# Weight-conversion units, attention bursts and fold fetches placed anew in a one-core chain of retention and two MoE layers

## The chip, the cores and the metric

The kernel runs on one core of a Trainium2 chip. The metric is device time in microseconds, the median of the runs; a profiled execution gives the trace. The engines are named PE (matrix multiply; PEld its weight loads), DVE (vector), ACT (scalar activation), POOL (GpSimd) and SP (which here issues every DMA). SPq is SP's queue of DMA issues, L99 the one helper line from which all of them come.

## The reference

```
scores = matmul(q, k^T) / sqrt(64)             # 8 x 8 heads, 576 positions, width 64
ret    = matmul(scores * gamma^(i-j), v)       # lower triangle only
x      = ret as 4608 x 512
h      = max(x @ w1, x @ w2, x @ w3)           # moe,  512 -> 768
x      = h @ w_out                             # 768 -> 512
a, b   = x @ w1, x @ w2                        # moe2, 512 -> 1024
out    = ((a * b) @ w3) @ w_out                # 1024 -> 1024 -> 512
```

Weights arrive as float64 and are turned into float32 words on the chip.

## The kernel before, in words

**First stage (to about 494 us).** Tokens go in 9 blocks of 512. For every block, 18 products (6 slices f of the hidden width, 3 weights i) of 12 matmuls each make `ps_h`; ACT copies the first of three into `hb`, DVE takes the maximum with the other two (L502), and `hb` is stored to `h_d`. One product is one tick of a list, `plan`: `when(t, fn)` puts a step at a time counted in ticks, the list is sorted, and every engine gets its instructions in that order and works through them strictly in order. Blocks 0 and 1 are written out by hand in the string `ORDER`, where a `+` takes the next step from the sorted list; tick 36 is where block 2 starts.

**Attention** is computed chunk by chunk in bursts of two chunks (`attend`, with `t_o` the tick at which a burst's outputs are made and `behind` that of the burst ahead of it, where its scores are made). A chunk fetches q and k (eight DMAs, L99), POOL scales q and v, DVE transposes them to `qt` and `kt` (L368), PE makes the scores `sc`, the outputs `o` and the new state `st`, DVE turns `st` into the state `s` (two instructions, L416 and L418) and masks the scores (`p`, L382). PSUM tiles `ps_h`, `sc` and `st` share six banks in turn, so a `sc` waits until the `hb` step has read the `ps_h` that had its bank six tiles before.

**Conversion units.** The late weights (moe w_out, moe2 w1, w2, w_out, w3) are 46 units of 512 KB. Each is fetched as raw words 6 ticks ahead (`fetch`), split by ACT (two instructions, L172 and L173), combined by DVE in three instructions (L177, L178 `CUSTOM_DVE`, L181; the order listing calls L178 ISA), and stored to DRAM. The last 16 units are moe2's w3, which is also transposed (L235) before its store to `w3t_d`. The queue of SP issues all of this in order, and a store waits there until DVE has made its data.

**Second stage.** After the moe product, w3 and w_out of moe2 are folded into one matrix (`ps_w`; operands `th`, `tl`, `oh`, `ol` are split from `raw`), then seven-product forms of the two moe2 products follow (`ps_x`, `ps_v`, `ps_y`); their operands, `t4l` among them, are split by the steps of `operands`, each low half being made by the engine that `split` names.

Of the kernel before, what the change touches and what calls it, by code (L numbers as in the profile page):

```python
# [22 lines left out]
P = 128  # L23
N1 = 512
KF1, KF2, KD = F1 // P, F2 // P, DM // P
EARLY = 2
# [13 lines left out]
ga8 pr0.9 ft14 xh7 lo10 ft15 xl7 kp0.2 ft16 up8 ou8 mx0.9 + + + pr0.10 xh8 xl8 + pr1.0 mx0.10 sl11 jn11 wo13 pr1.2  # L40
sl12 ft17 mx1.0 sl13 hi11 wo14 lo11 pr1.6 sl14 wo15 jn12 wo16 jn13 pr1.3 jn14 mx1.6 hi12 hi13 lo12 hi14 pr1.1 lo13
mx1.3 lo14 sl15 jn15 wo17 pr0.11 mx1.1 hi15 mx1.2 lo15 kp1.0 sl16 pr1.5 mx0.11 jn16 kp0.3 sl17 hi16 pr1.4 lo16 jn17
hi17 pr1.9 mx1.4 mx1.5 lo17 kp1.1 pr0.12 mx1.9 pr1.7 mx0.12 + + + mx1.7 + + + + pr1.8 + + + + + + pr0.15 mx1.8 + + +
kp1.2 pr0.17 + + + + pr0.16 mx0.15 + mx0.16 + + mx0.17 kp0.5 + + + + + + + + pr0.14 + + + pr1.10 + + + + + + + +
pr0.13 mx1.10 pr1.12 mx0.13 + + mx0.14 + kp0.4 + + + + pr1.11 mx1.12 + + mx1.11 + + + kp1.3 + + + + + + + pr1.15 + + +
+ + + + + + + pr1.16 mx1.15 + + + + pr1.13 + + + + mx1.16 pr1.14 mx1.13 + + + + pr1.17 mx1.14 + kp1.4 + + + + + + +
mx1.17 + kp1.5 + + + + + + + + + + + + + + + + + + +
"""
BACC = dict(dynamic_dma_scratch_size=512)

# [37 lines left out]
def tile_retention_maxout_bilinear(ctx: ExitStack, tc, a, out):  # L88
    nc = tc.nc
# [8 lines left out]
    def load(dst, src):  # L98
        nc.sync.dma_start(out=dst, in_=src)  # L99
# [11 lines left out]
    w3t_d = dram.tile([P, KF2, KF2, P], F32, name="w3t_d")  # L111
# [42 lines left out]
    n_blk = NT // N1  # L154
    T_BLK = 3 * KF1


    def convert(t, loads, done, name=None):

        z = {}  # L160

        def fetch():
            z["raw"] = cv.tile([P, 1024], I32, tag="raw", name="raw", bufs=6)
            for dst, src in loads(z["raw"]):
                load(dst, src)

        def words():
            raw = z["raw"].rearrange("p (n t) -> p n t", t=2)
            z["hi"] = raw[:, :, 1]
            z["e"] = cv.tile([P, 512], F32, tag="e", name="e")  # L170
            z["r"] = cv.tile([P, 512], I32, tag="r", name="r")
            nc.scalar.activation(z["e"], raw[:, :, 1].bitcast(F32), AF.Copy, scale=2.0 ** -112)  # L172
            nc.scalar.activation(z["r"], raw[:, :, 0].bitcast(U32), AF.Copy, scale=2.0 ** -29)  # L173

        def scale():
            z["m"] = cv.tile([P, 512], I32, tag="m", name="m", bufs=4)
            nc.vector.tensor_scalar(z["m"], z["e"].bitcast(I32), 3, None, ALU.logical_shift_left)  # L177
            nc.vector.tensor_tensor(z["m"], z["m"], z["r"], ALU.add)  # L178

        def join():  # L180
            nc.vector.scalar_tensor_tensor(z["m"], z["hi"], -0x80000000, z["m"], ALU.bitwise_and, ALU.bitwise_or)  # L181
            z["w"] = z["m"].bitcast(F32)

        def finish():
            done(t, z["w"])

        if name is None:
            when(t - 6, fetch)
            when(t - 1, words)
            when(t, scale)  # L190
            when(t + 1, join)
            t += 2
            when(t, finish)
        else:
            for kind, fn in (("ft", fetch), ("wo", words), ("sl", scale), ("jn", join)):
                early(kind + name, fn)
            for kind, fn in (("hi", done[0]), ("lo", done[1])):
                early(kind + name, lambda fn=fn: fn(z["w"]))

    def words_of(name):  # L200
        return a[name].bitcast(I32)
# [21 lines left out]
    def rows_unit(t, src, dst):  # L223
        convert(t, lambda raw: [(raw, src)], lambda t, w: load(dst, w))

    def w3_unit(t, j, half):
        src = words_of("moe2_w3")[512 * half:512 * half + 512].rearrange("(b r) e -> r b e", r=32)

        def loads(raw):
            r = raw.rearrange("p (b e) -> p b e", e=64)  # L230
            return [(r[32 * e:32 * e + 32], src[:, :, 64 * (4 * j + e):64 * (4 * j + e) + 64]) for e in range(4)]

        def done(t, w):
            wt = cv.tile([P, 512], I32, tag="m", name="m", bufs=4).bitcast(F32)
            nc.vector.transpose(out=wt, in_=w)  # L235
            load(w3t_d[:, j, 4 * half:4 * half + 4], wt.rearrange("p (m i) -> p m i", i=P))

        convert(t, loads, done)

# [2 lines left out]
    rest = [lambda t, k=k: rows_unit(t, words_of("moe_w_out")[k * P:(k + 1) * P], wo1_d[:, k]) for k in range(KF1)]  # L242
# [2 lines left out]
        for i in range(2) for c in (0, 2, 1, 3) for half in range(2)]  # L245
    rest += [lambda t, k=k: rows_unit(t, words_of("moe2_w_out")[k * P:(k + 1) * P], wo2_d[:, k]) for k in range(KF2)]
    rest += [lambda t, j=j, half=half: w3_unit(t, j, half) for j in range(KF2) for half in range(2)]
    for u, add in enumerate(rest):
        add(EARLY * T_BLK - 4 + u * ((n_blk - 1 - EARLY) * T_BLK - 1) / len(rest))

# [216 lines left out]
    bursts = []  # L469
    for m in reversed(range(0, len(due), 2)):  # L470
        some = due[m:m + 2]
        t_o = min(some[-1][2], T_BLK * some[0][1] - 2.52, bursts[0][0] - 7 if bursts else NT)
        bursts.insert(0, (int(t_o + 0.52) - 0.52, some))
    behind = bursts[0][0] - 9
    for t_o, some in bursts:
        pair = {}
        for slot, (n, _, _) in enumerate(some):
            attend(n, behind, t_o, slot, pair)
        behind = t_o
# [28 lines left out]
    for t in range(n_blk):  # L508
        for f in range(KF1):
            for i in range(3):  # L510
                k = T_BLK * t + 3 * f + i
                if t < EARLY:
                    split = t == 0 and 3 * f + i < HALVED
# [16 lines left out]
    KH, half = KF1 // 2, DM // 2  # L530
# [104 lines left out]
    with tc.manual_schedule():  # L635
# [78 lines left out]
        steps = halves[0][:2] + halves[1][:1] + halves[0][2:] + halves[1][1:]  # L714
# [48 lines left out]
                    split()  # L763
            pending.append([get(n) for get, n in gets])

        first_34 = [((get_w3t, 0), (get_wo2, 0)), ((get_w3t, 1),), ((get_w3t, 2), (get_wo2, 1)), ((get_w3t, 3),)]

        def open_34():
            t34["p"] = t34x.enter_context(tc.tile_pool(name="t34", bufs=2, side="left"))
# [19 lines left out]
        for j, (_, _, _, size) in enumerate(z_groups):  # L789
# [25 lines left out]
            if j == 3:  # L815
# [4 lines left out]
                steps = [lambda gets=gets: prepare_34(*gets) for gets in first_34]  # L820
# [11 lines left out]
        behind = []  # L832
# [13 lines left out]
        def operands(j, dst, c):  # L846

            w, size = {}, z_groups[j][3]

            def fetch():  # L850
                lows()
                r = raw_z()[:, :, :, :size]
                for kk in range(2):
                    load(r[:, kk], z_d[j][:, 2 * kk + c].rearrange("p (e t) -> p e t", e=2))
                for e in range(2):
                    for kk in range(2):
                        w[f"b{kk + 1}{e + 1}"] = r[:, kk, e]

            def split(x, src, eng):
                h, l = (v[:, c, columns(size)] for v in ops[dst][x])  # L860
                w_src = w[src]
                copy_r(h, w[src])
                behind.append(lambda: low(eng, l, w_src, h))

            def sub(x, y, to=None):
                if to is None:
                    t = spare_z()[:, :size]
                else:
                    t = w[to]
                nc.vector.tensor_tensor(t, w[x], w[y], ALU.subtract)  # L870
                return t

            def diff(dst, x, y, to=None):
                if to:
                    lows()
                w[dst] = sub(x, y, to)

            return [fetch,
                    lambda: (split("b11", "b11", nc.gpsimd), diff("t3", "b22", "b12")),
                    lambda: split("b21", "b21", nc.gpsimd),  # L880
                    lambda: diff("t1", "b12", "b11", "b12"),
                    lambda: diff("t2", "b22", "t1"),
                    lambda: split("t1", "t1", nc.vector),
                    lambda: split("t2", "t2", nc.vector),
                    lambda: diff("t4", "b21", "t2", "b21"),
                    lambda: split("t3", "t3", nc.vector),
                    lambda: split("b22", "b22", nc.vector),
                    lambda: split("t4", "t4", nc.gpsimd)]

        def waiting():  # L890
            pass
# [7 lines left out]
        rest = []  # L899

        def fetches(j):
            steps = both(j)
            rest.append(steps[2:])
            return steps[:2]
# [2 lines left out]
            return [lambda two=steps[n:n + 2]: [step() for step in two] for n in range(0, len(steps), 2)]  # L907

        one, two = fetches(0)
        steps = [waiting, waiting, one, waiting, waiting, two] + rest.pop() + fetches(1) + 3 * [waiting]  # L910
        w4x = ctx.enter_context(ExitStack())
        w4_p = t34["late"] = w4x.enter_context(tc.tile_pool(name="w4", bufs=4, side="right"))
        ps_w = []
        for n in range(2 * KF2):
            k, e = divmod(n, 2)
# [215 lines left out]
        for n, (k, q) in enumerate(visits):  # L1131
            B, size = ops[k % 2], z_groups[k][3]
            if n == 5:
                steps = steps + fetches(visits[7][0])
            elif n == 9:
                steps = steps + late[1]
            elif n != 4:
                steps = steps + rest.pop()
# [41 lines left out]
            for o in (2 * q, 2 * q + 1):  # L1180
# [3 lines left out]
                def add(ps, x, y, start):  # L1184
                    for i in range(2):
                        (ah, al), (bh, bl) = wsum[i][q][x], B[y]
                        product(ps[i][:, :size], [(ah[:, c, fs], al[:, c, fs], bh[:, c, columns(size)], bl[:, c, columns(size)]) for c in range(2)],
                                start, True, not start)
# [134 lines left out]
```

## Time and profile before

| | |
|---|---|
| median of 3 runs | 1223.95 us (1223.43 to 1228.09) |
| profiled execution | 1223.12 us, span of its instructions 1221.4 us |
| PE busy | 1208.2 us, 99% of the span |
| DVE, ACT, POOL busy | 906.2, 506.1, 311.9 us |
| mean granted PE clock | 0.999 of full speed |

Idle time of an engine that is not the bottleneck costs nothing by itself. Matmul ends are modelled, so the places where PE really stood still are read from the waits and the timeline of PE.

### The profile page before, as it was taken

The numbers are of one execution on the slowest core, as the hardware profiler recorded it, in microseconds if no ns is written. First come the engines' busy times: TensorE is split into PE (matmuls) and PEld (weight loads), VectorE is DVE, ScalarE is ACT, GpSimd is POOL, SyncE is SP. The second block draws the span as 40 slices with busy tenths as digits, with TensorE's granted clock in tenths as the row PEclk, the third lists the DMA queues.
The fourth block names the chain that finished last, engine by engine and source line by source line (L and its number), as shares of the span: only waits on it lengthen the run. The fifth ranks groups of instructions, "written<-read, shape, count | busy, mean of one in ns | idle before, by whom it ended". The sixth has DMA issues, their size and how long they took to land.

```text
span 1221.4 us, 22975 instructions
## 1 busy us (share of the span) xinstructions
PE 1208.2 (99%) x8900; PEld 1078.7 (88%) x8900; DVE 906.2 (74%) x1256; ACT 506.1 (41%) x873; POOL 311.9 (26%) x262
## 2 busy tenths in 40 slices
PE   8999999999999989999999999999999999999999
PEld 6888888888888878888889888888998888999998
DVE  5996677777877767366998467876666777998996
ACT  4651222233222322234556454443443344555554
POOL 2211221121211110000000125545244442344443
PEclk9999999999999999999999999999999999999999
DMA  9955788887998787444753733333333314455553
GB/s 219 252 127 121 161 204 230 196 213 180 223 221 172 168 172 192 146 128 165 227 185 122 251 112 130 129 121 119 107 115 136 128 59 159 155 165 166 176 169 104
DMA packets 323793, 199.34 MB, mean 163 GB/s; under 512 B 241634, under 2 KB 279266, under 8 KB 323684
## 3 DMA queue, kind: packets, MB, share of 16 engines
q1 hardware_dynamic: 323684, 197.87, 57.9%
q8 instruction: 70, 1.15, 0.4%
q14 instruction: 39, 0.32, 0.1%
HBM read 131.76 MB, written 66.06 MB: 162 GB/s over the span
## 4 chain that ended last, share of the span: by engine, by line
PE 88%; DVE 3%; DMA 3%; SPq 3%; issue 1%; POOL 1%; ACT 1%; DVEq 0%; POOLq 0%; ACTq 0%
PE ps_h L492 29%; PE ps_x L723 22%; PE ps_y L723 11%; PE ps_v L723 6%; PE ps_X L723 5%; PE ps_w L723 3%; SPq L99 3%; PE ps_Y L723 3%; PE o L390 2%; PE sc L375 2%; PE ps_V L723 1%; PE st L410 1%; PE o L397 1%; DMA q<-in_q_dram 1%; DMA raw<-in_moe_w_dram 1%
## 5 line engine op out<-in xcount | busy, mean ns | idle before, releaser
L492 PE MATMUL ps_h<-xh,w1h 128*128 128x512 f32 (+1 forms) x664 | 250.2, 378 | 0.0
L492 PE MATMUL ps_h<-xh,w1l 128*128 128x512 f32 (+1 forms) x664 | 247.4, 374 | 0.0
L492 PE MATMUL ps_h<-xl,w1h 128*128 128x512 f32 (+1 forms) x664 | 167.1, 374 | 0.0
L492 PEld LDWEIGHTS ps_h<-xh,w1h 128*128 128x128 f32 x664 | 125.5, 189 | 19.7 <-issue 2.1
L492 PEld LDWEIGHTS ps_h<-xh,w1l 128*128 128x128 f32 x664 | 125.6, 189 | 16.8 <-issue 0.3
L492 PEld LDWEIGHTS ps_h<-xl,w1h 128*128 128x128 f32 x664 | 123.7, 189 | 16.9
L1177 POOL TENSOR_TENSOR c<-c 128x512 f32<-128x512 f32 (+1 forms) x60 | 83.3, 1389 | 164.8 <-DVE c L1169 127.4
L502 DVE TENSOR_TENSOR hb<-ps_h,hb 128x512 f32<-128x512 f32 (+1 forms) x110 | 74.4, 677 | 62.8 <-PE ps_h L492 59.1
L1164 ACT ACTIVATE snap<-ps_x 128x512 f32<-128x512 f32 (+1 forms) x100 | 55.3, 554 | 151.4 <-PE ps_x L723 139.7
L361 POOL TENSOR_TENSOR q<-q,tables 128x512 f32<-128x512 f32 (+1 forms) x31 | 31.7, 1023 | 295.5 <-DMA q<-in_q_dram 224.9
L93 ACT ACTIVATE hb<-ps_h 128x512 f32<-128x512 f32 (+1 forms) x56 | 32.7, 584 | 173.7 <-PE ps_h L492 171.5
L172 ACT ACTIVATE e<-raw 128x512 f32<-128x512 f32 x64 | 54.1, 845 | 52.3 <-DMA raw<-in_moe_w_dram 35.4
L93 ACT ACTIVATE xh<-o 128x512 fp32r<-128x512 f32 (+1 forms) x40 | 22.1, 552 | 116.2 <-PE o L397 77.9
L368 DVE STREAM_TRANSPOSE qt<-q 128x512 f32<-128x512 f32 (+1 forms) x31 | 40.8, 1315 | 29.4 <-POOL q L361 29.4
L364 POOL TENSOR_TENSOR v<-v,tables 128x512 f32<-128x512 f32 x40 | 45.6, 1142 | 61.7 <-DMA v<-in_v_dram 44.4
L382 DVE TENSOR_TENSOR p<-sc,mask 128x512 f32<-128x512 f32 (+1 forms) x80 | 48.0, 627 | 11.2 <-PE sc L375 11.1
L178 DVE CUSTOM_DVE_ANT_0 m<-m,r 128x1024 uint16<-128x1024 uint16 x64 | 48.2, 753 | 6.9 <-ACT r L173 0.2
L96 POOL TENSOR_TENSOR ol<-raw,oh 128x512 fp32r<-128x512 f32 x1 | 1.3, 1265 | 203.7 <-DMA raw<-w3t_d 203.7
L173 ACT ACTIVATE r<-raw 128x512 int32<-128x512 uint32 x64 | 53.2, 831 | 0.0
L181 DVE SCALAR_TENSOR_TENSOR m<-raw,m 128x512 int32<-128x512 int32 x64 | 50.7, 796 | 0.2
L1169 DVE TENSOR_TENSOR c<-ps_x,snap 128x512 f32<-128x512 f32 (+1 forms) x40 | 25.1, 634 | 32.6 <-ACT snap L1164 13.3
L368 DVE STREAM_TRANSPOSE kt<-k 128x512 f32<-128x512 f32 (+1 forms) x31 | 41.0, 1324 | 8.7 <-DMA k<-in_k_dram 8.6
(302 smaller groups left out, 3257.9 us busy)
## 6 DMA issues: line engine op xcount, KB each, us to landing
zr<-g_d SPq DMA_DIRECT2D x18, 1024.0 KB, 6.1
raw<-in_moe_w_dram SPq DMA_DIRECT2D x34, 512.0 KB, 5.8
g_d<-c SPq DMA_DIRECT2D x64, 256.0 KB, 2.2
zr<-z_d SPq DMA_DIRECT2D x28, 512.0 KB, 6.5
h_d<-hb SPq DMA_DIRECT2D x54, 256.0 KB, 3.5
b<-h_d SPq DMA_DIRECT2D x16, 768.0 KB, 5.9
out_dram<-ob SPq DMA_DIRECT2D x35, 256.0 KB, 2.1
v<-in_v_dram SPq DMA_DIRECT2D x32, 256.0 KB, 4.7
```

What stands on the lines that cost most here:

```text
L93: nc.scalar.activation(dst, src, AF.Copy)
L172: nc.scalar.activation(z["e"], raw[:, :, 1].bitcast(F32), AF.Copy, scale=2.0 ** -112)
L173: nc.scalar.activation(z["r"], raw[:, :, 0].bitcast(U32), AF.Copy, scale=2.0 ** -29)
L178: nc.vector.tensor_tensor(z["m"], z["m"], z["r"], ALU.add)
L181: nc.vector.scalar_tensor_tensor(z["m"], z["hi"], -0x80000000, z["m"], ALU.bitwise_and, ALU.bitwise_or)
L368: nc.vector.transpose(out=z[x + "t"][:, :, :c].rearrange("p h (t T) -> p T h t", T=r), in_=z[x][:, :r])
L382: nc.vector.tensor_tensor(z[g][:c, :, :c], z["sc"][g][:c, :, :c], mask[:c, :c].unsqueeze(1).to_broadcast([c, G, c]), ALU.mult)
L492: nc.tensor.matmul(ps[:, cols], l, r, start=n == 0, stop=n == len(mms) - 1)
L502: nc.vector.tensor_tensor(hb, unwoven(ps[:, cols]), hb, ALU.max)
L723: nc.tensor.matmul(ps, l, r, start=start and j == 0, stop=stop and j == len(mms) - 1, skip_group_check=again)
L1164: nc.scalar.activation(t, unwoven(ps[:, :size]), AF.Copy)
L1177: nc.gpsimd.tensor_tensor(x, x, y, ALU.mult)
```

## The change

Four things. The late units start at tick 18.5 in place of 32 and end at about the same tick; a unit of w3 gets five parts of the stretch where the others get four (3.0 ticks against 2.4; all had 2.33). A unit of w3 is fetched by one DMA with pieces of 1 KB instead of four with pieces of 256 bytes; DVE's transpose writes its output in another order, and the store becomes four DMAs of 32 partitions. A burst comes at most 8 ticks behind the one ahead of it: from tick 51.48 to 131.48 the bursts stand 8 ticks apart, where gaps of 11, 7, 9, 7, 8, 9, 7, 7, 7, 8 ticks stood. In the fold, `wo2` 1 is fetched one step earlier, the second fetch of the first moe2 operands too, and the low halves of `t4` in the first group are made on DVE instead of POOL.

```
-hi17 pr1.9 mx1.4 mx1.5 lo17 kp1.1 pr0.12 mx1.9 pr1.7 mx0.12 + + + mx1.7 + + + + pr1.8 + + + + + + pr0.15 mx1.8 + + +
+hi17 pr1.9 mx1.4 mx1.5 lo17 kp1.1 pr0.12 mx1.9 pr1.7 mx0.12 + + + mx1.7 + + + + + pr1.8 + + + + + + + pr0.15 mx1.8 + +
...
     def w3_unit(t, j, half):
-        src = words_of("moe2_w3")[512 * half:512 * half + 512].rearrange("(b r) e -> r b e", r=32)
+        src = words_of("moe2_w3")[512 * half:512 * half + 512, 256 * j:256 * j + 256].rearrange("(p b) e -> p b e", b=4)
 
         def loads(raw):
-            r = raw.rearrange("p (b e) -> p b e", e=64)
-            return [(r[32 * e:32 * e + 32], src[:, :, 64 * (4 * j + e):64 * (4 * j + e) + 64]) for e in range(4)]
+            return [(raw.rearrange("p (b e) -> p b e", b=4), src)]
 
         def done(t, w):
             wt = cv.tile([P, 512], I32, tag="m", name="m", bufs=4).bitcast(F32)
-            nc.vector.transpose(out=wt, in_=w)
-            load(w3t_d[:, j, 4 * half:4 * half + 4], wt.rearrange("p (m i) -> p m i", i=P))
+            nc.vector.transpose(out=wt.rearrange("p (e r b) -> p b e r", e=4, b=4), in_=w.rearrange("p (b e) -> p b e", b=4))
+            for m in range(4):
+                load(w3t_d[:, j, 4 * half + m].rearrange("(e i) r -> i e r", i=32),
+                     wt[32 * m:32 * m + 32].rearrange("p (e r) -> p e r", e=4))
...
+    costs = [4] * (len(rest) - 2 * KF2) + [5] * 2 * KF2
     for u, add in enumerate(rest):
-        add(EARLY * T_BLK - 4 + u * ((n_blk - 1 - EARLY) * T_BLK - 1) / len(rest))
+        add(T_BLK + 0.5 + sum(costs[:u]) * (T_BLK * (n_blk - 2) - 6) / sum(costs))
...
     for t_o, some in bursts:
+        t_o = min(t_o, behind + 8) if behind > 0 and t_o != bursts[0][0] else t_o
         pair = {}
...
-        first_34 = [((get_w3t, 0), (get_wo2, 0)), ((get_w3t, 1),), ((get_w3t, 2), (get_wo2, 1)), ((get_w3t, 3),)]
+        first_34 = [((get_w3t, 0), (get_wo2, 0)), ((get_w3t, 1), (get_wo2, 1)), ((get_w3t, 2),), ((get_w3t, 3),)]
...
-                    lambda: split("t4", "t4", nc.gpsimd)]
+                    lambda: split("t4", "t4", nc.gpsimd if j else nc.vector)]
...
-        steps = [waiting, waiting, one, waiting, waiting, two] + rest.pop() + fetches(1) + 3 * [waiting]
+        steps = [waiting, waiting, one, waiting, two] + rest.pop() + fetches(1) + 3 * [waiting]
```

PE's own order stays as it was up to the burst at tick 51.48. Before it, the other engines get the early units between their old instructions. On SP's queue, in the stretch that leads to the bursts at ticks 21.48 and 29.48 (names on the left are destinations; `raw<-in_moe_w_out` is a unit's fetch, `wo_d<-m` its store), before:

```order
L99 DMA kn<-in_k_dram 128x8x64
L99 DMA q<-in_q_dram 32x16x32 x4
L99 DMA k<-in_k_dram 32x16x32 x4
L99 DMA h_d_65<-hb 128x512
L99 DMA v<-in_v_dram 128x8x64
L99 DMA kn<-in_k_dram 128x8x64
L99 DMA h_d_64<-hb 128x512
L99 DMA q<-in_q_dram 32x16x32 x4
```

and now, from the same `kn` to the same `q`:

```order
L99 DMA kn<-in_k_dram 128x8x64
L99 DMA raw<-in_moe_w_out_dram 128x1024
L99 DMA q<-in_q_dram 32x16x32 x4
L99 DMA k<-in_k_dram 32x16x32 x4
L99 DMA raw<-in_moe_w_out_dram 128x1024
L99 DMA h_d_65<-hb 128x512
L99 DMA raw<-in_moe_w_out_dram 128x1024
L99 DMA wo_d<-m 128x512
L99 DMA v<-in_v_dram 128x8x64
L99 DMA kn<-in_k_dram 128x8x64
L99 DMA h_d_64<-hb 128x512
L99 DMA q<-in_q_dram 32x16x32 x4
```

Three fetches and one store stand here that were not there; one more fetch stands ahead of these rows, and a fourth fetch of this kind and a second store follow before the next chunk's q and k (32x8x32).

On DVE, at the end of the same stretch, from the transposes of the 64-row chunk to the states `s` of the burst at tick 29.48, before:

```order
L368 STREAM_TRANSPOSE qt<-q 128x2x4x32
L368 STREAM_TRANSPOSE kt<-k 128x2x4x32
L502 TENSOR_TENSOR hb<-ps_h,hb 128x512
L416 TENSOR_TENSOR s<-st,s 128x256
L418 TENSOR_TENSOR s<-s,tables 128x256
```

and now (its lines are two to three numbers higher):

```order
L370 STREAM_TRANSPOSE qt<-q 128x2x4x32
L181 SCALAR_TENSOR_TENSOR m<-raw,m 128x512
L370 STREAM_TRANSPOSE kt<-k 128x2x4x32
L177 TENSOR_SCALAR m<-e 128x512
L178 ISA m<-m,r 128x1024
L181 SCALAR_TENSOR_TENSOR m<-raw,m 128x512
L505 TENSOR_TENSOR hb<-ps_h,hb 128x512
L418 TENSOR_TENSOR s<-st,s 128x256
L420 TENSOR_TENSOR s<-s,tables 128x256
```

A whole unit's three instructions now stand between the last transpose and the maximum and states behind it. One burst earlier, between the transposes and the maxima (L502) that the queue's `h_d_64` above waits for, the same three kinds stand too.

On SP's queue around a unit of w3, before:

```order
L99 DMA raw<-in_moe_w_dram 32x16x64 x4
L99 DMA h_d_69<-hb 128x512
L99 DMA q<-in_q_dram 32x8x32 x4
L99 DMA k<-in_k_dram 32x8x32 x4
L99 DMA w3t_d<-m 128x512
```

and now:

```order
L99 DMA raw<-in_moe_w_dram 128x4x256
L99 DMA h_d_69<-hb 128x512
L99 DMA v<-in_v_dram 128x8x64
L99 DMA kn<-in_k_dram 128x8x64
L99 DMA q<-in_q_dram 32x8x32 x4
L99 DMA k<-in_k_dram 32x8x32 x4
L99 DMA w3t_d<-m 32x4x128 x4
```

A unit still takes five issues, one fetch and four stores instead of four and one.

## Rows read from the trace of the kernel before

**Rows 1.** The page's first section: busy time and share of each engine.
```profile
PE 1208.2 (99%) x8900; PEld 1078.7 (88%) x8900; DVE 906.2 (74%) x1256; ACT 506.1 (41%) x873; POOL 311.9 (26%) x262
```

**Rows 2.** The timeline of PE, late bursts: start, duration, what, [idle before, releaser].
```profile
417.59 1.10 PE L375 MATMUL sc<-qt,kt 64*64 64x128 f32 x30 [0.80 <-DVE hb L502]
419.55 0.46 PE L397 MATMUL o<-qt,s 64*64 64x64 f32 x16 [0.86 <-DVE s L418]
...
440.80 0.69 PE L410 MATMUL st<-v,kn 128*64 128x64 f32 x16 [1.86 <-POOL v L364]
...
447.61 0.67 PE L397 MATMUL o<-qt,s 64*64 64x128 f32 x16 [1.27 <-DVE s L418]
```

**Rows 3.** Busy times in a stretch, the clock granted behind POOL's column.
```profile
440.00:460.00 20.00, 17.93 (x183) 15.74 (x184) 16.03 (x26) 4.66 (x7) 3.03 (x3) 0.91 0.83 187
```

**Rows 4.** Waits of PE: line, releaser, us in total, times, longest.
```profile
PE ps_x L723 <- POOL t4l L96: 0.7, 2, 0.4
...
PE ps_w L723 <- POOL ol L96: 0.5, 1, 0.5
```

**Rows 5.** Timelines of POOL and DVE at the late bursts.
```profile
438.70 1.05 POOL L361 TENSOR_TENSOR q<-q,tables 128x512 f32<-128x512 f32 x1 [8.50 <-DMA q<-in_q_dram]
...
414.56 1.13 DVE L368 STREAM_TRANSPOSE kt<-k 128x512 f32<-128x512 f32 x1 [0.65 <-DMA k<-in_k_dram]
```

**Rows 6.** Issues on SP's queue, all of L99: ns min/median/max.
```profile
L99 SPq DMA_DIRECT2D q<-in_q_dram x142: 457/634/2601, 2.2 to 453.6; - x142
...
L99 SPq DMA_DIRECT2D raw<-in_moe_w_dram x98: 368/536/1958, 7.5 to 474.4; - x98
...
L99 SPq DMA_DIRECT2D w3t_d<-m x16: 319/433/2808, 385.3 to 491.9; - x16
...
L99 SPq DMA_DIRECT2D raw<-in_moe_w_out_dram x14: 342/450/3760, 130.9 to 335.4; - x14
L99 SPq DMA_DIRECT2D wo_d<-m x14: 319/410/3562, 153.2 to 366.0; - x14
```

**Rows 7.** The chain that ended last, eight products: start, duration, what.
```profile
448.28 20.92 PE ps_h L492 x96
```

**Rows 8.** DVE's groups by form: count, busy us, mean ns, idle before.
```profile
L181 DVE SCALAR_TENSOR_TENSOR m<-raw,m 128x512 int32<-128x512 int32 x64 | 50.7, 796 | 0.2
L178 DVE CUSTOM_DVE_ANT_0 m<-m,r 128x1024 uint16<-128x1024 uint16 x64 | 48.2, 753 | 6.9 <-ACT r L173 0.2
...
L368 DVE STREAM_TRANSPOSE kt<-k 128x512 f32<-128x512 f32 x25 | 38.1, 1523 | 4.9 <-DMA k<-in_k_dram 4.8
...
L177 DVE TENSOR_SCALAR m<-e 128x512 int32<-128x512 int32 x64 | 27.9, 436 | 0.2
...
L235 DVE STREAM_TRANSPOSE m<-m 128x512 f32<-128x512 f32 x16 | 11.2, 703 | 0.1
```

**Rows 9.** The timeline of SP's queue, 113 to 131 us.
```profile
113.64 0.70 SPq L99 DMA_DIRECT2D kn<-in_k_dram  x1
117.69 0.34 SPq L99 DMA_DIRECT2D h_d<-hb  x1
...
128.26 2.59 SPq L99 DMA_DIRECT2D k<-in_k_dram  x4
```

**Rows 10.** The timeline of DVE, 114 to 136 us.
```profile
114.55 1.57 DVE L368 STREAM_TRANSPOSE kt<-k 128x512 f32<-128x512 f32 x1
116.25 1.42 DVE L502 TENSOR_TENSOR hb<-ps_h,hb 128x512 f32<-128x512 f32 x2
...
132.89 0.55 DVE L368 STREAM_TRANSPOSE kt<-k 128x256 f32<-128x256 f32 x1 [1.64 <-DMA k<-in_k_dram]
...
135.59 0.42 DVE L418 TENSOR_TENSOR s<-s,tables 128x256 f32<-128x256 f32 x1
```

**Rows 11.** The timeline of PE at the two early bursts.
```profile
118.92 1.93 PE L375 MATMUL sc<-qt,kt 64*64 64x128 f32 x64
...
138.47 0.33 PE L397 MATMUL o<-qt,s 64*64 64x128 f32 x2
```

More of the change, by code (lines that the diff above doesn't have):

```diff
@@ L42 @@
 mx1.3 lo14 sl15 jn15 wo17 pr0.11 mx1.1 hi15 mx1.2 lo15 kp1.0 sl16 pr1.5 mx0.11 jn16 kp0.3 sl17 hi16 pr1.4 lo16 jn17
-hi17 pr1.9 mx1.4 mx1.5 lo17 kp1.1 pr0.12 mx1.9 pr1.7 mx0.12 + + + mx1.7 + + + + pr1.8 + + + + + + pr0.15 mx1.8 + + +
[L44 to L47, printed above, removed]
+hi17 pr1.9 mx1.4 mx1.5 lo17 kp1.1 pr0.12 mx1.9 pr1.7 mx0.12 + + + mx1.7 + + + + + pr1.8 + + + + + + + pr0.15 mx1.8 + +
++ + + kp1.2 pr0.17 + + + + + + + + + + pr0.16 mx0.15 + mx0.16 + + mx0.17 kp0.5 + + + + + + + + + + + pr0.14 + + +
+pr1.10 + + + + + + + + + + + + + + + pr0.13 mx1.10 pr1.12 mx0.13 + mx0.14 + kp0.4 + + + + + + + + pr1.11 mx1.12 + + +
++ mx1.11 + + + kp1.3 + + + + + + + + pr1.15 + + + + + + + + + + pr1.16 mx1.15 + + + + + + + pr1.13 + + mx1.16 pr1.14
+mx1.13 + + + + + pr1.17 mx1.14 + kp1.4 + + + + + + mx1.17 + kp1.5 + + + + + + + + + + + + + + + + + + +
 """
```

## The prediction

> **What bounds the kernel now.** I read the page's first section, then who PE waited for, then the timeline of PE where it waited, and only then the engines that released it. PE is busy 99% of the span [rows 1], so apart from its own work (which the change leaves as it is, matmul for matmul) only what PE loses can be won. It loses little, in few places. Four waits stand at two late bursts of attention: 0.80, 0.86, 1.86 and 1.27 us, 4.79 us together [rows 2]. The clock granted right there is 0.91 of full over 20 us [rows 3], that is, some of it at the lower of the two levels, 1.2 GHz; before it fell PE had stood 1.86 us and run short attention matmuls. At 0.91 the stretch loses 0.09 x 20 = 1.8 us. Two more places are in the second stage: 0.7 us for `t4l` from POOL and 0.5 us for `ol` from POOL [rows 4]. That the late waits come from the queue of DMA issues shows one step behind them: POOL had idled 8.50 us until q landed, scaled it at 438.70, and only behind that could it scale the v that PE wanted; a burst earlier DVE's transpose had waited for k, with the maximum and the state that PE waited for queued behind it [rows 5].
>
> Why the queue is late there: a chunk's q and k take eight issues of 0.634 us, a burst of two chunks sixteen, 10.1 us [rows 6]. A w3 unit takes four fetches of 0.536 and a store of 0.433 us, 2.58 us [rows 6]. A tick is one product, 20.92 / 8 = 2.6 us [rows 7]. With bursts 7 ticks apart and a unit every 2.33 ticks, q, k and three units fill (10.1 + 7.7) / 7 = 2.55 us of every 2.6 us tick, and v, kn and `h_d` come on top; only the few us that PE spends in the burst itself pay for these. Three gaps of 7 stand in a row up to the second of these bursts.
>
> **The change part by part.**
>
> *Late bursts and w3.* With 8 ticks between bursts and a unit every 3 ticks there are 2.67 units to a gap. The fetch in one DMA of 1 KB pieces has the form of the first w1 fetches, which are in the row with the median of 0.536 us; a store of 32 partitions has no row. Its bounds are 0.319 us (the shortest store) and 0.634 us (a q issue, also 32 partitions, with more pieces) [rows 6]; I take 0.433, what a store costs now. A unit is then 0.536 + 4 x 0.433 = 2.27 us (1.81 to 3.07), and a tick of the queue needs (10.1 + 2.67 x 2.27) / 8 = 2.0 us (1.9 to 2.3). Even at the upper bound that is under 2.55. The transpose writes with a stride; its price lies between 0.703 us (the plain one, L235) and 1.523 us (`kt`, which is strided as well) [rows 8], at most 16 x 0.82 = 13 us more over 120 us on an engine that is busy 16 of 20 us at its fullest there [rows 3], and with the units spread wider it gets about as much back (46 units had 2.33 ticks each; these get 3.0). So it lies beside PE's products and costs nothing; without that cover it would delay each state by 0.8 us. I count the four waits and the clock as gone: -4.79 - 1.8 = -6.6 us. The lower bound is that half of the waits stay (below).
>
> *The fold.* `ol` of `wo2` 1 is fetched one step, at least one group of matmuls, earlier, against a wait of 0.5 us: gone. `t4l` moves to DVE behind `b22l`, where its two instructions stand ahead of four maxima-like sums that had to wait for PE anyway; POOL's long chain ahead of it goes: -0.7 us. Sum -1.2 us. The earlier second fetch of operands has the gap ahead of it as cover; if it pushed a fold operand back it would cost back the 0.5 us.
>
> *The early units.* This is where I see a price. Ticks are shorter than products before tick 36, as much of blocks 0 and 1 was done earlier: from the burst at 21.48 to that at 29.48, 8 ticks, PE goes from `sc` at 118.92 to `o` at 138.47 [rows 11], under 20 us instead of the 26 that 8 ticks and a burst take later. Units now fall into this stretch by the count of ticks. On the queue stand, ahead of the q and k of the second burst's 64-row chunk, five fetches of 0.450 and two stores of 0.410 us [rows 6]; with 0.05 us between issues, 3.4 us. What could swallow that is one wait of the queue: `kn` ends at 114.34 and `h_d` starts at 117.69, 3.35 us later [rows 9]. But `h_d` waits for two maxima on DVE, 116.25 to 117.67 [rows 10], and those move too. Ahead of them DVE now has the transposes of a chunk whose fetch stands behind two more issues (+1.0 us) and three unit instructions, 0.796 + 0.436 + 0.753 = 1.98 us [rows 8]. So the maxima end at 117.67 + 1.0 + 1.98 = 120.65 and `h_d` goes out 3.0 us late; with one more fetch and store (0.96) the last k of that chunk, which ended at 130.85 [rows 9], is 4.0 us late. DVE's last transpose then ends at 133.44 + 4.0 = 137.4 [rows 10], behind it stand 1.98 us of unit, a maximum (0.68, from the pair of 1.42) and two state instructions of 0.42: the state is ready at 141.0, and PE wants it at 138.47 [rows 11]. New wait: 2.5 us, part of it already at 119.9, where the second half of the scores needs the bank that one of those maxima frees at 120.65. The bounds: nothing, if the extra issues take 0.32 us and the fetches' landing is not later; and 2.5 + 1.8 = 4.3 us if PE's wait takes the clock down as at 440 us. I take 2.5. Behind it PE itself is late by as much, so the queue has its margin back; for the two gaps of 7 ticks that stay (to ticks 44.48 and 51.48) with their units I add 0.5 us (0 to 2.5, the same wait once more).
>
> The Trainium skill speaks against this term. "DMA: Bandwidth & Descriptors", section "Issuing engines are not separate DMA queues", calls the sequencer's time to initiate a DMA usually small relative to the DMA itself. By that the seven early issues would cost the queue nothing that matters, and the sum would be without the 3.0 us; the row of q, where 0.634 us of issue repeat sixteen times in every burst, disagrees with it here.
>
> Sum: -6.6 - 1.2 + 2.5 + 0.5 = -4.8 us against the profiled execution's 1223.12 (its span of 1221.4 and 1.7 us around it, which I leave alone), that is 1218.3; the median of the runs shown stands 0.83 above that execution, so **1219.1 us**.
>
> **The rivals.** *The queue has room (no early wait).* The early issues are hidden, as the skill's rule has it: -7.8 us, 1216.2. For it: ahead of tick 36 the queue has a wait of 3.35 us. Against it: that wait ends on DVE, which gets work as well.
>
> *The late waits stay in part.* DVE's unit instructions, not the queue, hold the states, and the longer transposes add to them: half of 4.79 and of 1.8 stays, -4.8 + 3.3 = -1.5, 1222.4. For it: at 419.55 the state stood behind unit instructions. Against it: those stood behind a transpose that waited for k [rows 5].
>
> *Slower.* The early lateness never recovers up to tick 51.48: the 2.5 us and the clock's 1.8 us are lost at each of the five bursts from 21.48 to 51.48, +21.5 - 7.8 = +13.7, 1237.6. It decides where a gap of 7 ticks leaves the queue less than its three units' (0.450 + 0.410 + 0.1) x 3 = 2.9 us. Against it: units at nearly this density stood in the same gaps before, with no such waits.
>
> *The moved bursts change nothing*, since the waits depend on w3 alone, gives the first or second rival's time and has no chance of its own.
>
> **How the numbers follow.** Forecast (late waits gone, an early wait of 2 to 4 us): 0.55, 1217.3 to 1220.8. No early wait: 0.25. Late waits stay in part: 0.14. Slower: 0.06. The range, 1215.8 to 1222.8, takes in both neighbours and leaves out the slow case, the second rival's upper part and a clock lost on top of everything. 0.5% is 6.1 us, about what a measurement of this kernel can tell from no change. Faster by more (below 1217.8) is the first rival and an eighth of the forecast: 0.31. Slower by more is the last rival but for a rest where fewer bursts lose: 0.05; within: 0.64.
>
> **What would show it.** Right: in PE's waits no `st` behind POOL's v and no `o` behind `s` after 400 us, no clock under 0.99 there; a wait of `sc` or `o` of 1 to 3 us between 118 and 143 us; no wait for `t4l` in 720 to 740 or for `ol` near 682; w3's fetch issued once in about 0.5 us, its four stores in under 0.5 each. Wrong: no early wait (the term of 2.5 falls), an early wait repeated at each burst to 210 us (the slow rival), late waits on `s` with q and k landed in time (DVE, not the queue, was the cause), or a new PE wait in the fold.

## The result, and the profile after

The changed kernel took 1234.63 us (median of 5 runs, 1232.24 to 1237.41) beside 1225.37 us of the kernel before in the same comparison: ratio 1.0075, 95% interval 1.0052 to 1.0097. It is slower by 0.75%, where 1219.1 us, faster than before, was forecast. Its profiled execution took 1233.91 us, its span 1232.2.

The page's first section answers to [rows 1]: PE's share fell from 99% to 98%, and its busy time grew by 4.9 us although its work is the same.

```profile
PE 1213.1 (98%) x8900; PEld 1081.7 (88%) x8900; DVE 915.3 (74%) x1260; ACT 504.7 (41%) x873; POOL 308.6 (25%) x258
```

PE's longest waits (line, releaser, us in total, times, longest) answer to [rows 4]. Neither `t4l` nor `ol` is among its waits any more.

```profile
PE st L412 <- POOL v L366: 4.9, 3, 2.6
PE o L399 <- DVE s L420: 2.4, 3, 1.8
PE sc L377 <- DVE hb L505: 1.8, 2, 1.1
```

PE does the same matmuls in both kernels, so the start of the same `ps_h` matmul (number 157, 889 and 1549 of them) tells how late PE is. From the timeline of PE before:

```profile
68.53 0.48 PE L492 MATMUL ps_h<-xh,w1h 128*128 128x512 f32 x1
...
266.09 0.48 PE L492 MATMUL ps_h<-xh,w1h 128*128 128x512 f32 x1
...
450.90 0.38 PE L492 MATMUL ps_h<-xh,w1h 128*128 128x512 f32 x1
```

and after, with the attention matmuls of the two early bursts ([rows 11] before) and of the late one:

```profile
71.28 0.48 PE L495 MATMUL ps_h<-xh,w1h 128*128 128x512 f32 x1
...
124.08 1.10 PE L377 MATMUL sc<-qt,kt 64*64 64x128 f32 x30 [1.15 <-DVE hb L505]
...
141.53 0.69 PE L412 MATMUL st<-v,kn 128*64 128x64 f32 x16 [2.59 <-POOL v L366]
142.04 3.42 PE L392 MATMUL o<-p,v 128*64 128x128 f32 x32
...
280.99 0.38 PE L495 MATMUL ps_h<-xh,w1h 128*128 128x512 f32 x1
...
432.79 0.70 PE L399 MATMUL o<-qt,s 64*64 64x64 f32 x16 [1.81 <-DVE s L420]
...
463.34 0.38 PE L495 MATMUL ps_h<-xh,w1h 128*128 128x512 f32 x1
```

PE is 2.75 us late at the first of these starts, 14.90 at the second, 12.44 at the third, and 10.8 at the end. So the kernel loses 12.15 us between 68 and 266 us (of before's time), wins 2.46 up to 451, and 1.6 behind that. Lined up burst by burst, the 12.15 us are 1.6 at the burst of tick 21.48, 4.3 at 29.48, 1.6 at 37.48, 1.5 at 44.48, 2.6 at 51.48, and 0.6 at 67.48. The `o` of 32 matmuls at 142.04 took 3.42 us; the same 32 took 1.92 a burst earlier. The windows (busy times of PE, PEld, DVE, ACT and POOL, then PE's granted clock, DMA share, GB/s; [rows 3] before) show a clock of 0.91, so some time at the lower level of 1.2 GHz, at the early burst and near the late one. The first row is that of before, the other three are the changed kernel's:

```profile
75.00:270.00 195.00, 194.74 (x1767) 170.16 (x1766) 141.57 (x212) 56.10 (x84) 30.32 (x34) 1.00 0.75 184
```

```profile
75.00:270.00 195.00, 186.80 (x1604) 161.90 (x1594) 139.83 (x212) 60.80 (x91) 30.10 (x32) 0.99 0.76 185
140.00:160.00 20.00, 18.47 (x184) 16.49 (x185) 12.52 (x22) 6.32 (x9) 4.08 (x6) 0.91 0.82 208
430.00:450.00 20.00, 18.18 (x117) 15.61 (x118) 16.81 (x24) 5.15 (x8) 2.73 (x2) 0.91 0.83 189
```

Why `st` waited for v at 141.53 stands on POOL and on SP's queue. POOL had idled until the next burst's q landed, and this burst's v was scaled only behind it, the pattern of [rows 5], now at an early burst:

```profile
139.86 0.62 POOL L363 TENSOR_TENSOR q<-q,tables 128x256 f32<-128x256 f32 x1 [6.63 <-DMA q<-in_q_dram]
140.43 1.04 POOL L366 TENSOR_TENSOR v<-v,tables 128x512 f32<-128x512 f32 x1
```

SP's queue, to be read beside [rows 9]: the last k of the 64-row chunk began at 128.26 and now begins at 137.99. Behind the fetch at 118.14 the queue stood until DVE had made `wo_d`'s data, and then v took 1.57 us to issue, `h_d` 0.93, another `wo_d` 2.04:

```profile
118.14 0.38 SPq L99 DMA_DIRECT2D raw<-in_moe_w_out_dram  x1
122.29 0.33 SPq L99 DMA_DIRECT2D wo_d<-m  x1
122.71 1.57 SPq L99 DMA_DIRECT2D v<-in_v_dram  x1
...
125.00 0.93 SPq L99 DMA_DIRECT2D h_d<-hb  x1
126.03 2.64 SPq L99 DMA_DIRECT2D q<-in_q_dram  x4
...
133.26 2.04 SPq L99 DMA_DIRECT2D wo_d<-m  x1
...
137.99 3.57 SPq L99 DMA_DIRECT2D k<-in_k_dram  x4
```

The issues over the whole run (ns min/median/max; [rows 6] before) keep medians near those that the prediction used; w3's four stores take 0.446 each, under the 0.5 that it named:

```profile
L99 SPq DMA_DIRECT2D w3t_d<-m x64: 302/446/2413, 360.1 to 505.6; - x64
...
L99 SPq DMA_DIRECT2D raw<-in_moe_w_out_dram x14: 376/498/1892, 100.6 to 320.0; - x14
```

DVE's strided transpose of w3 by form ([rows 8] before) takes 1.4 us in place of 0.7, and at the late wait it stood between the transpose of k and the state (timeline of DVE):

```profile
L234 DVE STREAM_TRANSPOSE m<-m 128x512 f32<-128x512 f32 x16 | 22.5, 1408 | 0.0
...
428.19 1.11 DVE L370 STREAM_TRANSPOSE kt<-k 128x512 f32<-128x512 f32 x1 [0.53 <-DMA k<-in_k_dram]
...
429.74 1.12 DVE L234 STREAM_TRANSPOSE m<-m 128x512 f32<-128x512 f32 x1
...
432.31 0.42 DVE L420 TENSOR_TENSOR s<-s,tables 128x256 f32<-128x256 f32 x1
```

### The profile page after: what moved, and what is told of

Read it like the earlier page. It is cut to its first block, busy times and chain, and to the rows that moved or that the text cites. A ratio compares the mean times of both kernels' runs of the same rounds, so it can differ in the third digit from the quotient of the medians.

```text
span 1232.2 us, 22949 instructions
## 1 busy us (share of the span) xinstructions
PE 1213.1 (98%) x8900; PEld 1081.7 (88%) x8900; DVE 915.3 (74%) x1260; ACT 504.7 (41%) x873; POOL 308.6 (25%) x258
## 4 chain that ended last, share of the span: by engine, by line
PE 75%; SPq 4%; DVE 2%; DMA 2%; issue 1%; ACT 0%; POOL 0%; DVEq 0%; POOLq 0%; ACTq 0%
PE ps_x L726 22%; PE ps_h L495 19%; PE ps_y L726 11%; PE ps_X L726 6%; PE ps_v L726 6%; SPq L99 4%; PE ps_w L726 3%; PE ps_Y L726 3%; PE ps_V L726 1%; PE o L392 1%; PE sc L377 1%; PE st L412 1%; PE o L399 1%; DMA k<-in_k_dram 1%; DMA raw<-in_moe_w_dram 0%
```

## Experiments

For each run the table at the end of this section gives PE's lateness by stretch, worked out as above from the starts of the same four matmuls. Theory at the outset: the early units cost what was lost before 266 us, through SP's queue. Rivals: DVE's part of these units, and the edits of the late bursts.

**Which half of the change.** The changed kernel with the units' old ticks and old order string:

```
-        add(T_BLK + 0.5 + sum(costs[:u]) * (T_BLK * (n_blk - 2) - 6) / sum(costs))
+        add(EARLY * T_BLK - 4 + u * ((n_blk - 1 - EARLY) * T_BLK - 1) / len(rest))
```

> The changed kernel with the late units back at the ticks of before (from tick 32 on, 2.33 ticks each) and the order string of before; w3's 1 KB packets, the bursts at most 8 ticks apart and the fold's fetches stay as changed. Theory 'early units': the lateness that PE gathers between 75 and 223 us (11.6 us by the alignment of the two traces) is the work of the units between ticks 18.5 and 52, so it goes: 1219 to 1224 us, faster than before if the late waits are gone too. Rival 'late edits': the new form of w3 or the moved bursts cost the time: 1230 us or more.

Measured: ratio 0.9978 (0.9965 to 0.9990), faster than before; 1.10 us lost between 68 and 266 us. The kernel before with the new ticks and order string alone (the same lines the other way):

> The kernel before with only the units' new ticks (from 18.5 on, w3 units 3.0 ticks) and the new order string. Theory 'early units': the same 10 to 14 us of lateness by 225 us, and at 438 to 448 us at least part of the 5 us of late waits gone, as the units are spread wider there too: 1230 to 1238 us. Rival 'late edits': 1220 to 1226 us.

Measured: 1.0059 (1.0045 to 1.0074), 11.97 us lost. The early units are the loss, and the edits of the late bursts are not.

**Queue or DVE.** Fetches and stores of the first fourteen units issued by ACT:

```
+                (nc.scalar.dma_start(out=dst, in_=src) if early_unit else load(dst, src))
...
+            (nc.scalar if t < 54 else nc.sync).dma_start(out=dst, in_=w)
```

> The changed kernel with the fetches and stores of the first fourteen units (ticks 18.5 to 52) issued by ACT in place of SP; nothing else moved. Theory 'queue' (SP's issues hold q, k and v back): the waits of PE at the bursts of ticks 21.48 to 51.48 are gone, 1221 to 1226 us. Rival 'DVE' (the units' three vector instructions hold transposes, maxima and states back): the waits stay within 2 us in sum, 1232 to 1237 us.

And the first fourteen units without their vector instructions:

```
+            nc.scalar.activation(z["w"], z["raw"].rearrange("p (n t) -> p n t", t=2)[:, :, 1].bitcast(F32), AF.Copy, scale=2.0 ** -112)
...
-            when(t, scale)
-            when(t + 1, join)
```

> The changed kernel without the vector work of the first fourteen units: ACT's scaled copy of the high words is stored as it is, so moe w_out and half of moe2 w1 are left unconverted and the outputs are not the reference's; all their DMAs stay. Theory 'queue': the waits at the bursts of ticks 21.48 to 51.48 stay for the most part, 1230 to 1236 us. Rival 'DVE': they go, 1221 to 1226 us.

Measured: 1.0058 (1.0036 to 1.0081) with 8.96 us lost, and 1.0070 (1.0052 to 1.0088) with 12.19 us lost. Both theories as I had put them fell: the loss stays without the issues on SP's queue, and it stays without DVE's work. (The first of the two is not clean: ACT stood at stores until DVE had made their data, and 4.87 of the 8.96 us fell at tick 21.48.) Issues of SP were long in both, though no early fetch stood in SP's queue in the first. Its queue, where the four issues of a chunk's q or k took 0.634 us each [rows 6], 2.5 together:

```profile
127.58 3.79 SPq L99 DMA_DIRECT2D q<-in_q_dram  x4
131.76 5.25 SPq L99 DMA_DIRECT2D k<-in_k_dram  x4
```

and the queue and PE of the second:

```profile
120.58 2.51 SPq L99 DMA_DIRECT2D h_d<-hb  x1
123.18 3.59 SPq L99 DMA_DIRECT2D q<-in_q_dram  x4
...
139.82 0.69 PE L418 MATMUL st<-v,kn 128*64 128x64 f32 x16 [3.23 <-POOL v L372]
```

An `h_d` that usually takes some 0.4 us took 2.51. That suggested a third theory: what the early fetches cost is not their issue but their 512 KB.

**Is the profile repeatable, and does the head of the queue matter.** The changed kernel once more, unchanged:

> The changed kernel as it is, for a second profile and for its time on the chip of the next three. If the 2.4 us that PE lost at 427 to 433 us in the first profile, and the 1.9 us at 59 to 71 us, belong to the change, they stand at the same places again; if they are chance, at least one is missing. 1.006 to 1.010 of the kernel before.

Measured: 1.0060 (1.0041 to 1.0078). It lost 2.07 us before 68 us and 10.47 between 68 and 266, again most of it at tick 29.48 (`st` waited 3.13 us for v at 140.17); the wait of 1.8 us near 432 was missing (0.3), so it does not come in every execution. The same with each early store one unit later:

```
+            held.append(lambda: done(t, z["w"]))
+            while len(held) > (t < 54):
+                held.pop(0)()
```

> The changed kernel with the store of each of the first fourteen units one unit (2.4 ticks) later; all else stays. Theory 'head of the queue' (SP stands at a store until DVE has made its data, with v, h_d and the next q and k behind it; 3.8 us at 118.5 to 122.3): that wait goes, and the burst at tick 29.48 is late by 2 to 4 us less; over the five bursts 4 to 8 us are won. Rival 'density' (each unit's issues, transfers and vector work cost whatever their order): within 2 us of the changed kernel.

Measured: 1.0075 (1.0053 to 1.0097), 11.01 us lost: the head of the queue is not it.

**Bytes.** The kernel without early vector work, with an eighth of the bytes in as many DMAs of as many pieces:

```
+                    dst, src = dst[:, :128], src[:, :128]
...
+            load(dst[:, :64], w[:, :64])
```

> As the kernel without the early units' vector work, but each of its early fetches and stores moves an eighth of the bytes, in the same number of issues (so still more of the weights is left unconverted, and constants are stored there later; the outputs are not the reference's). Theory 'transfers' (the 512 KB fetches keep the eight DMAs that may be under way from landing, so SP's issues behind them take 2 us and more): most of the 10 us that the kernel without vector work lost at the bursts of ticks 29.48 and 44.48 goes, 7 us or more. Rival 'issues' (it is the time of the issues themselves): less than 4 us goes.

Measured: one run, 1218.93 us beside 1222.01; the loss is gone (-0.51 us against 12.19). Its row for 75 to 270 us, and behind it that of the kernel without early vector work, which differs in the bytes, in the width of ACT's one instruction a unit, and in not storing constants 34 ticks later:

```profile
75.00:270.00 195.00, 195.00 (x1770) 170.79 (x1769) 129.63 (x189) 47.89 (x84) 31.42 (x37) 1.00 0.70 165
```

```profile
75.00:270.00 195.00, 187.40 (x1626) 163.50 (x1626) 116.45 (x172) 51.33 (x77) 29.11 (x32) 0.98 0.78 189
```

The other way round, ACT's and DVE's part of these units kept, the fetches left out, and the stores made later from a constant:

> The changed kernel with the scalar and vector work of the first fourteen units at its places, on constant data, but without their fetches, and with their stores made of constants 36 ticks later (so moe w_out and part of moe2 w1 are not converted and the outputs are not the reference's). If SP's queue is what makes PE late, the five bursts lose under 2 us in sum up to 225 us. If DVE's instructions alone do it, they lose 7 us or more. If each hides the other, 3 to 6.

Measured: one run, 1220.45 us; nothing lost (-0.51). And all work kept at its place, with only the bytes cut to an eighth (the two lines above on the changed kernel, ACT and DVE working on a constant tile, and constants stored later):

> The changed kernel with every instruction at its place, but the early units' fourteen fetches and fourteen stores move an eighth of the bytes (64 KB in place of 512, 32 in place of 256); ACT and DVE do the units' full work on other data, and constants are stored in those places later, so the outputs are not the reference's. Theory 'bytes' (the transfers of the early units hold up the fetches of q, k and v behind them, DVE's work is covered): of the 10 to 12 us that PE loses between 75 and 266 us, under 2 us stay; about 1218 to 1222 us. Rival 'DVE too': 4 to 8 us stay, 1224 to 1228 us.

Measured: 0.9994 (0.9984 to 1.0004), 0.70 us lost. Of the changed kernel's early loss nearly all goes with the bytes.

**Which bytes.** Only the fetches cut, only the stores cut, and both by half:

> As the run with an eighth of the bytes, but only the fourteen early fetches are cut; the fourteen early stores move their full 256 KB (weights are left unconverted, so the outputs are not the reference's). If the fetches alone hold q, k and v up: under 2.5 us lost between 75 and 266 us. If fetches and stores add up by their bytes (512 to 256): 3 to 4 us.

> As the run with an eighth of the bytes, but only the fourteen early stores are cut; the fetches move their full 512 KB (weights are left unconverted and constants stored later, so the outputs are not the reference's). If the fetches alone are to blame: 8 us or more are lost between 75 and 266 us. If fetches and stores add up: 6 to 8 us. If there is a threshold that only both together pass: under 3 us.

> As the run with an eighth of the bytes, but with half of them (256 KB a fetch, 128 KB a store; the outputs are not the reference's). If the loss grows with the bytes: 4 to 6 us between 75 and 266 us. If there is slack that must first be used up: under 2.5 us.

Measured, one run each: 1216.39, 1235.17 and 1229.71 us beside 1222.35, with -0.03, 6.67 and 3.92 us lost between 68 and 266 us. With small fetches nothing is lost, full stores and all. With full fetches and small stores 6.67 us are lost, less than the 10.5 to 12.2 with full stores; by the bounds set beforehand that is the case in which fetches and stores add up. Half of the bytes cost about a third of the loss, which is between the two cases set beforehand. (The table has what the last two runs lost outside this stretch.)

Split by burst (starts of the matmuls 157, 397, 445 and 721), the loss has two parts. At tick 29.48 every one of the seven profiles with early fetches of 512 KB lost 3.7 to 6.0 us, the one with small stores 3.85 among them; half of the bytes lost 2.79, an eighth -0.13, 0.35 and 1.08. That part goes with the fetches' bytes. The bursts at 37.48, 44.48 and 51.48 together lost 3.6 to 6.5 us with all bytes and all issues on SP, 1.59 with small stores, 0.29 with the DMAs on ACT, and -0.5 with half of the bytes.

With small fetches, all instructions in the same order and full stores, SP's queue reads:

```profile
117.59 0.33 SPq L99 DMA_DIRECT2D wo_d<-m  x1
118.01 0.39 SPq L99 DMA_DIRECT2D v<-in_v_dram  x1
...
120.07 0.34 SPq L99 DMA_DIRECT2D h_d<-hb  x1
120.51 3.18 SPq L99 DMA_DIRECT2D q<-in_q_dram  x4
...
128.27 0.77 SPq L99 DMA_DIRECT2D wo_d<-m  x1
...
131.74 2.58 SPq L99 DMA_DIRECT2D k<-in_k_dram  x4
```

Against the changed kernel's rows above v issues in 0.39 us, not 1.57, `h_d` in 0.34, not 0.93, the second `wo_d` in 0.77, not 2.04, and the last k begins 6.3 us earlier, of which 1.9 are PE's smaller lateness at 68 us. It is not always the same issues that are long: with full fetches and small stores v and `h_d` took 0.39 and 0.34 us as well (at 120.69 and 122.76), but the second `wo_d` 1.97 and the last k began at 136.05. POOL's q follows the queue, and the window of 75 to 270 us shows PE busy throughout:

```profile
133.49 0.61 POOL L373 TENSOR_TENSOR q<-q,tables 128x256 f32<-128x256 f32 x1 [5.26 <-DMA q<-in_q_dram]
...
75.00:270.00 195.00, 194.75 (x1768) 170.64 (x1767) 154.63 (x230) 66.78 (x97) 33.94 (x38) 1.00 0.72 172
```

What lands is slower than with small fetches as well, but not slower than before. Transfers between 100 and 220 us (KB each, median us from issue to landing) of the changed kernel, then with small fetches, then before:

```profile
h_d<-hb SPq DMA_DIRECT2D x11, 256.0 KB, 4.8
v<-in_v_dram SPq DMA_DIRECT2D x9, 256.0 KB, 5.2
```

```profile
h_d<-hb SPq DMA_DIRECT2D x11, 256.0 KB, 3.6
...
v<-in_v_dram SPq DMA_DIRECT2D x9, 256.0 KB, 4.1
```

```profile
h_d<-hb SPq DMA_DIRECT2D x11, 256.0 KB, 5.1
...
v<-in_v_dram SPq DMA_DIRECT2D x8, 256.0 KB, 5.0
```

**What the kernel before shows of the same thing.** Before has long issues behind large fetches too. Its queue, just behind [rows 9]:

```profile
130.94 0.55 SPq L99 DMA_DIRECT2D raw<-in_moe_w_out_dram  x1
...
132.06 0.38 SPq L99 DMA_DIRECT2D raw<-in_moe_w_out_dram  x1
...
134.75 2.20 SPq L99 DMA_DIRECT2D h_d<-hb  x1
```

These stand behind the last k of the 64-row chunk (128.26), and PE did not wait at that burst. Between the matmuls 157 and 889 before issues 20 fetches of late units and the changed kernel 23, and the DMA share from 75 to 270 us is 0.75 and 0.76 (rows above). So the number of large fetches in the stretch is nearly the same; what differs at tick 29.48 is that five of them stand ahead of that last k, where none stood. No run moved these five alone.

**The other parts, one at a time on the kernel before.** The bursts at most 8 ticks apart, the new w3 unit, and the fold's edits, each with its lines of the diff:

> The kernel before with the bursts at most 8 ticks apart, and nothing else of the change. If the gaps of 7 ticks make the late waits (438 to 448 us), these 5 us go: ratio about 0.996. If it is the form of w3's fetches, they stay: 1.000.

> The kernel before with the new fetch, transpose and four stores of a w3 unit, and nothing else of the change. By the prediction's budget of the queue (2.27 us a unit in place of 2.58) a unit every 2.33 ticks and gaps of 7 ticks leave 2.4 us of every 2.6: the late waits go in part, 0.997 to 0.999. If the strided transpose costs DVE the 0.8 us it might, they grow: over 1.000.

> The kernel before with the fold's fetches moved and t4's low half of the first group on DVE, and nothing else of the change. The prediction's term: -1.2 us, ratio 0.999; the two waits for t4l and the one for ol are gone from PE's waits. The late waits at 438 to 448 us stay.

Measured: 1.0017 (1.0001 to 1.0033), 0.9979 (0.9966 to 0.9991), 0.9983 (0.9973 to 0.9993). The last two together:

> The kernel before with the new w3 unit and the fold's new fetches, units and bursts at their old ticks. If the two gains that the single runs showed (ratios 0.9979 and 0.9983) are separate places, they add up: 0.996 to 0.997, faster than all kernels here. If the gain of the w3 unit was chance of the late waits: 0.998 to 0.999.

Measured: 0.9981 (0.9972 to 0.9991). The gains did not add up, and the ratio is the one expected for a w3 gain by chance; in its profile PE waited 0.9 us for `ol`, now from DVE:

```profile
PE ps_w L724 <- DVE ol L96: 0.9, 1, 0.9
```

Four versions are faster than the kernel before, by 0.17 to 0.22%, and are not told apart: the change without early units, the w3 unit alone, the fold alone, and these two together.

PE's lateness against the profile of before in us, by stretch (before's time):

```
                                  to 68   68-266  266-451  from 451
changed                           2.75    12.15    -2.46    -1.61
changed, again                    2.07    10.47    -6.90    -0.64
changed, later stores             1.72    11.01    -5.87    -1.84
before + early units              1.95    11.97    -7.34    -0.48
DMAs on ACT                       2.94     8.96    -6.86    -1.48
no vector work                    1.85    12.19    -5.45    -0.91
no vector work, 1/8 of bytes      2.36    -0.51    -5.52    -0.63
no early fetches, stores later    1.78    -0.51    -2.52    -1.42
1/8 of bytes                      0.67     0.70    -3.15    -0.94
1/8 in fetches only               0.86    -0.03    -6.52    -1.00
1/8 in stores only                2.41     6.67     1.94     0.93
1/2 of bytes                      4.71     3.92    -1.05    -1.09
changed, late units               1.75     1.10    -4.61    -2.03
before + bursts 8 apart           2.38     0.91    -0.81    -0.09
before + w3 unit                  0.76    -0.08    -4.47     0.02
before + fold                     1.65     0.64    -3.87    -1.91
before + w3 unit + fold           1.44    -0.51    -4.21     0.01
```

## Why the prediction was wrong, step by step

**The early units (+2.5 and +0.5) failed, and they decide the sign.** The place was right: SP's queue is late ahead of the bursts at ticks 21.48 and 29.48, and PE waits there, with the lower clock behind it. That tick 29.48 lost 4.3 us, the upper bound, was luck: the bound was worked out from another wait, and the second profile lost 6.0 us there. The step that failed is the price of a moved fetch: "five fetches of 0.450 and two stores of 0.410 us [rows 6]". That is its issue. Its 512 KB were costed at nothing (a later landing was named only as what the lower bound leaves out), although before's trace had the 2.20 us of `h_d` behind two such fetches. The runs show the reverse: all issues, stores and vector work together cost -0.03 us when only the fetches are small, and 10.5 to 12.2 when they are not. The last k, forecast 4.0 us late, began 9.73 us later, 7.0 beyond the 2.75 of PE's own lateness. Who waited longest at tick 29.48 was also read wrongly: not `o` for DVE's state but `st` for POOL's v, which stands behind q of the next burst.

**"Behind it PE itself is late by as much, so the queue has its margin back"** fell too. The three bursts behind lost 1.6, 1.5 and 2.6 us more, 5.7 against the 0.5 counted for two of them. In kind that was the rival named *slower*, but that its 1237.6 is near 1234.6 is chance: it lost 4.3 us at each of five bursts and won all 7.8. Its condition, a gap that leaves the queue less than three units' issues, was the wrong one, since with small fetches the same issues stand there and nothing is lost. The reason against it, "units at nearly this density stood in the same gaps before", is true (about three fetches to a gap in both kernels) and did not save the forecast. Why these gaps cost time now, and did not before, is not shown; with half of the bytes they cost nothing.

**The Trainium skill's rule.** I set q's sixteen issues of 0.634 us against "DMA: Bandwidth & Descriptors", section "Issuing engines are not separate DMA queues" of the Trainium skill, which calls the time to initiate a DMA usually small relative to the DMA itself. The row of q was no test of that: beside the 0.634 us of its issue a q fetch took 4.0 us to land (median before, 100 to 220 us). For the early units the runs agree with the page: the issues cost -0.03 us. The first rival took from it that nothing would be lost, which does not follow. The same section says that DMAs from the scalar, sync and gpsimd engines run on the same 16 DMA engines and interleave; the run with the early DMAs on ACT, which still lost 8.96 us, fits that, though it is not clean.

**The late waits (-6.6) were mis-sized.** The profiles of the changed kernel show 2.46 and 6.90 us won in this stretch. But the fold alone, which touches nothing there, shows 3.87: its profile, of the same first stage, has 2.9 us of waits at the late bursts in place of 4.79, and the clock there is 1.00, not 0.91 [rows 3]:

```profile
440.00:460.00 20.00, 17.91 (x190) 15.69 (x191) 17.48 (x27) 4.67 (x7) 3.14 (x4) 1.00 0.86 200
```

So more than half of the 6.6 us belonged to one execution, not to the kernel. By the medians the change without early units (0.9978) is 0.05% beyond the fold alone (0.9983), some 0.6 us, with intervals wider than that. Alone, w3's new unit helped (0.9979) and the 8 ticks did not (1.0017). The transpose, costed at nothing behind a cover, took 0.70 us more each time; it stands in one late wait of the first profile. Whether it cost anything there was not tried.

**The fold (-1.2) was right**: the waits for `t4l` and for `ol` from POOL are gone, and the median fell by 0.17%, 2.1 us (0.9 to 3.3). In two profiles with it (the changed kernel's second, and w3 unit with fold), the 0.9 us for `ol` from DVE is the cost back that the text had named at 0.5.

**The 2.75 us before 68 us** are no part of the change: kernels that alter nothing there show 0.67 to 4.71, and the profile of before happened to have the quickest start.

What stays open: where a fetch of 512 KB holds up the issues behind it. That the loss goes with the fetches' bytes is shown, and that issues behind large fetches can be long; the place inside is not. The loss is not in proportion to the bytes either (10.5 to 12.2 us with all, 3.9 with half), as if slack were used up first; that rests on one run.

## What to carry to other kernels

A DMA that is moved has two prices: its issue on the queue, and its bytes, which here slowed the issue and the landing of transfers behind it. The trace before the change can show the second: look at the issues behind such a DMA where it stands now, and at who will stand behind it at its new place. The mean DMA share of the stretch told nothing here. An experiment that keeps every instruction and cuts only the bytes tells the two apart in one run. Waits that one profile shows at a few bursts are a sample: before counting them as a gain, look whether another execution of the same work has them.

## What was unexpected on the hardware

An `h_d` of 256 KB that issued in 0.34 us where the early fetches were small took 2.51 us behind two of 512 KB (2.20 before). Four k issues took 5.25 us although the large fetches were issued by another engine (5.13 for four at 196.25 us before, with all on SP). And DVE's transpose with a strided output took 1408 ns a time, against 703 ns with the plain one [rows 8].
